# Casting v inside the load: GpSimd DMAs write bf16 into the block-diagonal operand of a windowed attention, ones on both sides of a row

## The chip, the cores and the metric

One core of one Trainium2 chip. The metric is the device time of one execution in microseconds, as the median of several runs. The profile is of one execution; its span runs from the first to the last instruction of the core.

## The reference

A causal sliding-window attention with a linear distance bias, followed by a spectral mixing over the sequence.

```python
# q, k, v: 8 batches, 8 heads, 576 tokens, 64 wide; fp32
scores = scale * q @ k.T                       # per batch and head
bias   = slopes[h] * -abs(i - j)               # slopes 2 ** (-(h + 1))
mask   = (i - j >= 0) & (i - j < 128)
attn   = softmax(where(mask, scores + bias, -1e9))
x      = (attn @ v) with heads side by side    # 8 x 576 x 512
X      = rfft(x, axis=1)[:, :64]               # 64 modes
Y      = X[:, m] @ (w_r[m] + 1j * w_i[m])      # a 512 x 512 pair for each mode
u      = x + irfft(Y, n=576)
out    = u + relu(u @ w_ch)                    # fp32
```

The 128 weight matrices w_r, w_i are 1 MB each in fp32, 134 MB together; q, k and v are 9.4 MB each, and so is the output.

## The kernel before

**Units and stages.** Attention works on 16 units, each one batch and four heads. The order on every engine is written out by hand: `STAGE` lists the steps of one stage with a lag in units, and the loop over stages runs through it, so that several units are in work at once. In one stage the casts of k run two units ahead, those of q three ahead, and the value matmuls and the norm one behind.

**Steps of a unit.** `load` issues DMAs from SP into fp32 buffers, two for each of q, k and v. `cast` turns them into bf16 on VectorE and issues the load of the unit two further on. q and k are transposed on PE (L250) and copied out by ScalarE (L256). `score` multiplies them (L284), `exp` runs on ScalarE (L294), `mask` multiplies two of the four tiles on VectorE (L305). `value` (L331) multiplies the exponentials with v; `norm` (L346, L347) takes the reciprocal of the row sums and scales the result into x. The accumulator `av` of the value matmuls has one buffer. `spectrum` and `channels` transform x into the modes, XC.

**The value operand.** Keys are taken in pairs of 128-key blocks, two keys to a partition (j = 0, 1). For a pair of blocks the operand vb has 2 x W columns with W = D + 2 = 66: partitions 0 to 63 hold v in the first W columns and zeros in the second, partitions 64 to 127 the other way round. Behind the 64 columns of v stand two columns of ones, so that the row sum comes out of the same matmul. The last 64 keys have an operand of their own, vt. `fixtures` writes the zeros and ones once, on GpSimd; the casts of v (L233 for both halves, L235 for the tail) write only the v columns. There are two vb and two vt.

**Loads of v.** Five DMAs a unit from SP: four with one head each (L208, 128 partitions, 2 runs of 512 bytes) and one for the tail (L212). They stand in SP's queue between the loads of q and k.

**Weights during attention.** `load_w` with bf16 issues a GpSimd DMA that reads fp32 and writes bf16. One such weight goes out per stage into the pool `early` (`AHEAD`, `EARLY` = 14 buffers); ahead of it GpSimd copies one element of x into `gate` (L533), which makes it wait for the norm of the stage. At the end of attention seven more weights go into the freed fp32 buffers of q, k and v (`spare`, `LATER`).

**The weight stream.** After attention the other weights come as fp32 from SP (L465) into `NWA` = 6 buffers and later `NWB` = 2 more; PE takes the upper halves of the fp32 words as bf16 (L838). Eight of the early buffers are loaded a second time by GpSimd (`AGAIN`). The inverse transform, the projection with w_ch and the outputs run beside it and at its end.

Of the kernel before, what the change touches and what calls it, by code (L numbers as in the profile page):

```python
# [10 lines left out]
FP32 = mybir.dt.float32  # L11
BF16 = mybir.dt.bfloat16
# [23 lines left out]


STAGE = (
    ("exp", 1, 0), ("score", 0, 0), ("exp", 0, 0), ("value", 0, 1), ("spectrum", None, 2),
    ("cast", "v", 0), ("score", 2, 0), ("channels", None, 2), ("transpose", "k", -1),  # L40
# [66 lines left out]
class _Attention:  # L107


    def __init__(self, tc, ctx, q, k, v, consts, x, XC, raw):  # L110
        self.tc, self.nc = tc, tc.nc
        self.q, self.k, self.v = q, k, v
        self.ident, self.F, self.FT = consts
        self.x, self.XC = x, XC
        B, H, S, _ = q.shape
        self.S, self.NG = S, H // 4
        self.units = [(b, g) for b in range(B) for g in range(self.NG)]
        self.raw = raw
        self.mid = ctx.enter_context(tc.tile_pool(name="amid", bufs=2))
        self.ps = ctx.enter_context(tc.tile_pool(name="aps", bufs=1, space=PSUM))  # L120
        fix = ctx.enter_context(tc.tile_pool(name="afix", bufs=1))
        self.table = fix.tile([P, H, 2, 2 * P], BF16, name="mask")
        self.bias = fix.tile([P, H, 2, 2 * P], BF16, name="bias")
        self.vb = [fix.tile([P, 2, 4, 2, 2 * W], BF16, name=f"vb{i}") for i in range(2)]
        self.vt = [fix.tile([P, 4, 2, W], BF16, name=f"vt{i}") for i in range(2)]
        self.qkT = [fix.tile([P, 2, 2, (FULL + 1) * P], BF16, name=f"qkT{i}") for i in range(2)]
        self.att = [fix.tile([P, FULL * 8 * P + 64], BF16, name=f"att{i}") for i in range(2)]
        self.loaded, self.casted, self.open = {}, {}, {}

    def fixtures(self, i):  # L130
        nc = self.nc
        for t, tail in ((self.vb[i], self.vt[i]),):
            for half in range(2):
                row = slice(64 * half, 64 * half + 64)
                c0 = W * half
                nc.gpsimd.memset(t[row, :, :, :, W - c0 : 2 * W - c0], 0.0)
                nc.gpsimd.memset(t[row, :, :, :, c0 + D : c0 + W], 1.0)
            nc.gpsimd.memset(tail, 0.0)
            nc.gpsimd.memset(tail[64:96, :, :, D:], 1.0)
        nc.gpsimd.memset(self.att[i][:, FULL * 8 * P :], 1.0)  # L140
# [57 lines left out]
    def load(self, w, u):  # L198
        nc = self.nc
        if u >= len(self.units):  # L200
            return
        b, g = self.units[u]
        hs = slice(4 * g, 4 * g + 4)
        if w == "v":
            t = self.raw[w][:, u % 2]
            sv = self.v[b, hs]
            for h in range(4):
                nc.sync.dma_start(  # L208
                    out=t[:, :2, h],
                    in_=sv[h, : FULL * P].rearrange("(r p j) d -> p r (j d)", r=2, j=2),  # L210
                )
            nc.sync.dma_start(  # L212
                out=t[64:96, 2],
                in_=sv[:, FULL * P :].rearrange("h (p j) d -> p h (j d)", j=2),
            )
        else:
            t = self.raw[w][:, u % 2]
            src = (self.q, self.k)["qk".index(w)][b, hs]
            nc.sync.dma_start(
                out=t.rearrange("p e j d -> p e (j d)"),  # L220
                in_=src.rearrange("(e h) (p j) d -> (h p) e (j d)", h=2, j=TPP),
            )
        self.loaded[w, u] = t

    def cast(self, u, w):

        nc = self.nc
        src = self.loaded.pop((w, u))
        if w == "v":
            src = src.rearrange("p s h (j d) -> p s h j d", j=2)  # L230
            for half in range(2):
                row = slice(64 * half, 64 * half + 64)
                nc.vector.tensor_copy(  # L233
                    self.vb[u % 2][row, :, :, :, W * half : W * half + D], src[row, :2])
            nc.vector.tensor_copy(self.vt[u % 2][64:96, :, :, :D], src[64:96, 2])  # L235
        else:
            dst = self.mid.tile([P, TPP, 2, D], BF16, tag=w, name=w)
            nc.vector.tensor_copy(dst.rearrange("p j e d -> p e j d"), src)
            self.casted[u, w] = dst
        self.load(w, u + 2)  # L240
# [66 lines left out]
    def value(self, u, e):  # L307
# [5 lines left out]
        att, vb, vt = self.att[u % 2], self.vb[u % 2], self.vt[u % 2]  # L313
        last = u == len(self.units) - 1 and e == 1
        av = self.ps.tile([P, 2, 512], FP32, tag="sc" if last else "av", bufs=2 if last else 1)
        for h in range(2):
            bank = av[:, h, : (FULL + 1) * W]
            todo = []
            for pair in range(2):
                rhs = [vb[:, pair, 2 * e + h, j] for j in range(2)]  # L320
                todo.append((pair, 0, 2 * pair, rhs))
                if pair == 1 and odd:
                    todo.append((pair, P, 3, [r[:, :W] for r in rhs]))
                    todo.append((pair, P - 64, 4, [r[:, W:] for r in rhs]))
                else:
                    todo.append((pair, P, 2 * pair + 1, rhs))
            todo.append((1, 192 - 64 * odd, 4, [vt[:, 2 * e + h, j] for j in range(2)]))
            for n, (pair, c0, qt, rhs) in enumerate(todo):
                for j in range(2):
                    o = (((2 * pair + h) * 2 + e) * 2 + j) * 256 + c0  # L330
                    nc.tensor.matmul(  # L331
                        bank[:, qt * W : qt * W + rhs[j].shape[1]],
                        lhsT=att[:, o : o + P], rhs=rhs[j],
                        start=(n == 0 and j == 0), stop=(n == len(todo) - 1 and j == 1),
                        skip_group_check=True,
                    )
        self.open["av", e, u] = av

    def norm(self, u, e):
# [6 lines left out]
        nc.vector.reciprocal(rec, tiles[:, :, :, D])  # L346
        nc.vector.tensor_tensor(  # L347
            out=self.x[:, b, :, cs].rearrange("p t (h d) -> p h t d", h=2),
            in0=tiles[:, :, :, :D],
# [50 lines left out]
def kernel(  # L400
# [14 lines left out]
    AHEAD = {stage: 1 for stage in range(1, 14)}  # L415
    LATER = {13: 2, 14: 2, 15: 3}
    EARLY, NWA, NWB, AGAIN = 14, 6, 2, 8
# [17 lines left out]
    raw["v"] = rawpool.tile([P, 2, 3, 4, 2 * D], FP32, name="vr")  # L435
    spare = [raw[w][:, i].rearrange("p e j d -> p (e j d)") for w in "qk" for i in range(2)]
    vflat = raw["v"].rearrange("p u s h d -> p (u s h d)")
    spare += [vflat[:, 2 * DM * i :] for i in range(3)]
    spare = [t[:, : 2 * DM].bitcast(BF16).rearrange("p (a e) -> p a e", a=4) for t in spare]
# [28 lines left out]
    with ExitStack() as actx:  # L468
        at = _Attention(tc, actx, q, k, v, (ident, F, FT), x, XC, raw)
        n = len(at.units)  # L470
        for w, u in (("q", 0), ("k", 0), ("q", 1), ("k", 1), ("v", 0), ("v", 1)):
            at.load(w, u)
# [19 lines left out]
        at.fixtures(0)  # L492
        load_w(1, early, True)
        next(table, None)
        at.fixtures(1)
        nc.gpsimd.memset(XC[:, 4 * NC * NM :], 0.0)
# [20 lines left out]
        run("cast", "v", 0)  # L517
# [461 lines left out]
```

## Time and profile before

| what | value |
|---|---|
| time of three runs | 444.14, 444.54 and 446.43 us, median 444.54 |
| span of the profiled execution | 441.7 us; its own time outside the span is not recorded, the median lies 2.8 us above it |
| PE busy | 332.8 us, 75% |
| DVE busy | 184.5 us, 42% |
| ACT busy | 162.1 us, 37% |
| POOL busy | 50.2 us, 11% |
| HBM read, written | 162.53 MB, 9.44 MB |
| attention | first q load at 0.74 us, last value matmul at 134 us |
| weight stream, first fp32 weight issued | 129.3 us |
| loads of v, median from issue to landing | 7.6 us |
| casted weights, median from issue to landing | 8.3 to 8.8 us |

Busy times are of each engine over the whole span; most of VectorE's and ScalarE's lies in the first third. A DMA that casts is counted by the bytes that it writes. "Landing" is the time at which the completion of a DMA is seen.

### The profile page before, as it was taken

Reading aid. Unit: us, or ns where it says so; the run is one execution under the profiler, and the core shown is the slowest. Engines: PE = TensorE matmul, PEld = TensorE weight load, DVE = VectorE, ACT = ScalarE, POOL = GpSimd, SP = SyncE. Lnnn points to the kernel's source line nnn. Section 1 sums busy time; section 2 is a strip of 40 time slices with the busy share of each in tenths; the row PEclk is TensorE's granted clock in tenths of the full one; section 3 lists DMA queues with packets and bytes.
Section 4 is the critical chain, followed back from the end, with each engine's and each line's share of the span. In section 5 each row is a group of like instructions: output and inputs, shape, how many; then the busy total and the mean of one; then the engine's idle time right before and its main releaser. Section 6 shows DMA issues by size and latency. Waiting matters only on the chain. (4 is left out here: it accounts for less than half of the span.)

```text
span 441.7 us, 8410 instructions
## 1 busy us (share of the span) xinstructions
PE 332.8 (75%) x3509; PEld 179.9 (41%) x3509; DVE 184.5 (42%) x332; ACT 162.1 (37%) x211; POOL 50.2 (11%) x107
## 2 busy tenths in 40 slices
PE   5589899879886454454545597999979999879982
PEld 4367677667664221121112133444434444333440
DVE  7789899887863200010000021332222223122694
ACT  6849899978960000000000011232222322101781
POOL 8711010101302200110000000000000000002500
PEclk9969999999998855555555569999999999999998
DMA  8999999999999999999999999999999999997498
GB/s 282 321 325 280 299 322 298 317 294 301 225 214 315 319 316 316 331 383 426 419 422 421 422 422 418 420 421 418 421 419 421 421 418 419 421 422 313 170 376 322
DMA packets 53209, 156.92 MB, mean 355 GB/s; under 512 B 4772, under 2 KB 23860, under 8 KB 40756
## 3 DMA queue, kind: packets, MB, share of 16 engines
q1 hardware_dynamic: 47860, 140.56, 82.2%
q0 software_dynamic: 5312, 15.84, 18.1%
q8 instruction: 27, 0.44, 0.4%
q14 instruction: 10, 0.08, 0.0%
HBM read 162.53 MB, written 9.44 MB: 389 GB/s over the span
## 5 line engine op out<-in xcount | busy, mean ns | idle before, releaser
L838 PE MATMUL acc<-w,XC 128*32 128x512 bf16 x456 | 93.1, 498 | 62.3 <-DMA w<-in_moe_w_r_dram 34.0
L838 PEld LDWEIGHTS <-XC 128*32 128x32 bf16 x508 | 39.4, 149 | 114.5 <-issue 100.1
L294 ACT ACTIVATE att<-sc 128x1024 bf16<-128x1024 f32 x64 | 64.1, 1032 | 10.7 <-PE sc L284 10.6
L604 ACT CAST ZW<-zw 128x512 bf16<-128x512 f32 x8 | 4.7, 585 | 147.6 <-PE zw L602 147.6
L331 PE MATMUL av<-vb,att 128*128 128x132 bf16 (+1 forms) x576 | 38.6, 218 | 10.9 <-DVE x L347 5.9
L331 PEld LDWEIGHTS <-att 128*128 128x128 bf16 x704 | 36.7, 99 | 16.3 <-DVE x L347 10.2
L576 DVE TENSOR_SCALAR yq<-acc 128x512 bf16<-128x512 f32 x14 | 9.6, 686 | 79.6 <-PE acc L838 79.6
L670 PE MATMUL my<-wch,xT 128*64 128x512 bf16 x288 | 34.5, 381 | 5.8 <-ACT x L701 4.3
L679 ACT CAST XW<-my 128x512 bf16<-128x512 f32 x36 | 19.3, 589 | 51.0 <-PE my L627 51.0
L651 DVE COPY xT<-tr 128x1024 bf16<-128x1024 bf16 x18 | 12.4, 691 | 55.0 <-PE tr L649 55.0
L256 ACT COPY qkT<-tp 128x1152 bf16<-128x1152 bf16 x30 | 33.5, 1116 | 2.8 <-PE tp L250 2.1
L616 POOL DMA_DIRECT2D Z<-yq x11 | 5.5, 511 | 217.4 <-issue 216.2
L347 DVE TENSOR_TENSOR x<-av,rec 128x640 bf16<-128x640 f32 x32 | 26.4, 824 | 1.1
L284 PE MATMUL sc<-qkT 64*64 64x256 bf16 (+2 forms) x640 | 25.1, 263 | 2.1 <-ACT qkT L256 1.2
L670 PEld LDWEIGHTS <-xT 128*64 128x64 bf16 x288 | 17.2, 109 | 21.7 <-issue 9.3
L794 DVE TENSOR_TENSOR o<-yy,r 128x1024 f32<-128x1024 f32 (+1 forms) x22 | 21.5, 1024 | 4.3 <-ACT r L770 3.2
L233 DVE CAST vb<-vr 64x1024 bf16<-64x1024 f32 x32 | 22.6, 708 | 0.2
L701 ACT CAST x<-my 128x512 bf16<-128x512 f32 x18 | 10.5, 585 | 33.0 <-PE my L627 33.0
L284 PEld LDWEIGHTS <-qkT 64*64 64x64 bf16 x640 | 14.5, 109 | 19.4 <-issue 16.3
L702 DVE CAST x<-my 128x512 bf16<-128x512 f32 x18 | 12.4, 691 | 23.4 <-PE my L627 23.4
L271 PE MATMUL sc<-bias,ident 128*128 128x512 bf16 x64 | 20.8, 409 | 1.3 <-ACT att L294 1.3
L305 DVE TENSOR_TENSOR att<-att,mask 128x1024 bf16<-128x1024 bf16 x32 | 20.6, 683 | 0.0
(130 smaller groups left out, 396.6 us busy)
## 6 DMA issues: line engine op xcount, KB each, us to landing
w<-in_moe_w_i_dram SPq DMA_DIRECT2D x49, 1024.0 KB, 17.9
w<-in_moe_w_r_dram SPq DMA_DIRECT2D x48, 1024.0 KB, 16.0
qr<-in_q_dram SPq DMA_DIRECT2D x16, 576.0 KB, 10.3
kr<-in_k_dram SPq DMA_DIRECT2D x16, 576.0 KB, 8.6
vr<-in_v_dram SPq DMA_DIRECT2D x64, 128.0 KB, 7.6
out_dram<-o SPq DMA_DIRECT2D x13, 512.0 KB, 4.5
w<-in_moe_w_r_dram POOLq DMA_DIRECT2D x12, 512.0 KB, 8.8
w<-in_moe_w_i_dram POOLq DMA_DIRECT2D x10, 512.0 KB, 8.3
```

The lines of the kernel that those rows point to most:

```text
L233: nc.vector.tensor_copy(self.vb[u % 2][row, :, :, :, W * half : W * half + D], src[row, :2])
L256: (self.nc.vector.tensor_copy if u < 2 and w == "q" else self.nc.scalar.copy)(dst.rearrange("q h (p j) -> q h p j", j=TPP), tp.rearrange(" ...
L271: nc.tensor.matmul(sc[:, e], lhsT=self.ident, rhs=self.bias[:, hv].rearrange("p j n -> p (j n)"), start=True, stop=False, skip_group_check ...
L284: nc.tensor.matmul(sc[64 * half : 64 * half + 64, e, j * 256 + c0 : j * 256 + c0 + n], lhsT=qkT[row, 1, h, k0 + j : k0 + P : 2], rhs=qkT[r ...
L294: self.nc.scalar.activation(self.att[u % 2][:, kt * 8 * P : (kt + 1) * 8 * P], sc.rearrange("p e n -> p (e n)"), AF.Exp, scale=1.0 / math. ...
L305: nc.vector.tensor_tensor(out=rows, in0=rows, in1=self.table[:, heads], op=ALU.mult)
L331: nc.tensor.matmul(bank[:, qt * W : qt * W + rhs[j].shape[1]], lhsT=att[:, o : o + P], rhs=rhs[j], start=(n == 0 and j == 0), stop=(n == l ...
L347: nc.vector.tensor_tensor(out=self.x[:, b, :, cs].rearrange("p t (h d) -> p h t d", h=2), in0=tiles[:, :, :, :D], in1=rec.unsqueeze(-1).br ...
L670: nc.tensor.matmul(mm[ROWS[half]], lhsT=lhsT, rhs=wch[:, dt], start=(dt == 0), stop=False, skip_group_check=True,)
L679: nc.scalar.copy(XW[:, j, n], mms[n])
L794: nc.vector.tensor_tensor(out=o[:, c], in0=yy[:, c], in1=r[:, c], op=ALU.add)
L838: nc.tensor.matmul(into[32 * (m % 4) : 32 * (m % 4) + 32], lhsT=XC[:, c0 : c0 + 31 * NM + 1 : NM], rhs=wq[t][a], start=(ri == 0 and a == 0 ...
```

## The change

v is no longer loaded as fp32 and cast on VectorE. GpSimd DMAs read fp32 from HBM and write bf16 straight into vb and vt, five a unit as before: one for each pair of blocks and half (64 partitions, four heads, 128 elements each) and one for the tail. So that a run of 128 elements (two keys) can stand in one piece, a row is now [1, v of key 0, v of key 1, 1], WV = 130 columns: the matmul of key 0 takes the first 65, that of key 1 the last 65, shifted by one column in the accumulator. The sums of the two keys then lie in columns 0 and 65 of W = 66, and `norm` adds them with a tensor_reduce before the reciprocal. vb has three buffers (NV) instead of two, held where the fp32 buffers of v were, and vt three. The load of unit u + 3 is issued behind the second half of the value matmuls of unit u. The fixtures of the three buffers are written ahead of their first loads. One weight more is loaded early (15 instead of 14, two in stage 7), the spare buffers are filled in other stages, and the fp32 buffers are split 5 and 3 instead of 6 and 2.

```diff
+NV = 3
+WV = 2 * D + 2
 STAGE = (
-    ("cast", "v", 0), ("score", 2, 0), ("channels", None, 2), ("transpose", "k", -1),
+    ("score", 2, 0), ("channels", None, 2), ("transpose", "k", -1),
...
-        self.vb = [fix.tile([P, 2, 4, 2, 2 * W], BF16, name=f"vb{i}") for i in range(2)]
-        self.vt = [fix.tile([P, 4, 2, W], BF16, name=f"vt{i}") for i in range(2)]
+        self.vb = raw["v"]
+        self.vt = [fix.tile([P, 4, WV], BF16, name=f"vt{i}") for i in range(NV)]
...
     def load(self, w, u):
...
         if w == "v":
-            t = self.raw[w][:, u % 2]
+            t = self.vb[:, u % NV]
             sv = self.v[b, hs]
-            for h in range(4):
-                nc.sync.dma_start(
-                    out=t[:, :2, h],
-                    in_=sv[h, : FULL * P].rearrange("(r p j) d -> p r (j d)", r=2, j=2),
-                )
-            nc.sync.dma_start(
-                out=t[64:96, 2],
+            for half in range(2):
+                row = slice(64 * half, 64 * half + 64)
+                for r in range(2):
+                    k0 = (2 * r + half) * P
+                    nc.gpsimd.dma_start(
+                        out=t[row, r, :, half, 1 : WV - 1],
+                        in_=sv[:, k0 : k0 + P].rearrange("h (p j) d -> p h (j d)", j=2),
+                    )
+            nc.gpsimd.dma_start(
+                out=self.vt[u % NV][64:96, :, 1 : WV - 1],
                 in_=sv[:, FULL * P :].rearrange("h (p j) d -> p h (j d)", j=2),
             )
+            return
...
     def cast(self, u, w):
-        if w == "v":
-            ...
-                nc.vector.tensor_copy(
-                    self.vb[u % 2][row, :, :, :, W * half : W * half + D], src[row, :2])
-            nc.vector.tensor_copy(self.vt[u % 2][64:96, :, :, :D], src[64:96, 2])
...
     def value(self, u, e):
...
+                m = rhs.shape[1]
+                dst = bank[:, qt * W : (qt + m) * W].rearrange("p (m w) -> p m w", w=W)
                 for j in range(2):
                     nc.tensor.matmul(
-                        bank[:, qt * W : qt * W + rhs[j].shape[1]],
-                        lhsT=att[:, o : o + P], rhs=rhs[j],
+                        dst[:, :, j : j + D + 1],
+                        lhsT=att[:, o : o + P], rhs=rhs[:, :, j * (D + 1) : (j + 1) * (D + 1)],
...
+        if e == 1:
+            self.load("v", u + NV)
     def norm(self, u, e):
-        nc.vector.reciprocal(rec, tiles[:, :, :, D])
+        nc.vector.tensor_reduce(out=rec, in_=tiles[:, :, :, 0 : D + 2 : D + 1],
+                                axis=mybir.AxisListType.X, op=ALU.add)
+        nc.vector.reciprocal(rec, rec)
...
-    AHEAD = {stage: 1 for stage in range(1, 14)}
-    LATER = {13: 2, 14: 2, 15: 3}
-    EARLY, NWA, NWB, AGAIN = 14, 6, 2, 8
+    AHEAD = {stage: 1 + (stage == 7) for stage in range(1, 14)}
+    LATER = {13: 2, 14: 3, 15: 1, 16: 1}
+    EARLY, NWA, NWB, AGAIN = 15, 5, 3, 8
...
-    raw["v"] = rawpool.tile([P, 2, 3, 4, 2 * D], FP32, name="vr")
+    raw["v"] = rawpool.tile([P, NV, 2, 4, 2, WV], BF16, name="vb")
...
-        for w, u in (("q", 0), ("k", 0), ("q", 1), ("k", 1), ("v", 0), ("v", 1)):
+        for w, u in (("q", 0), ("k", 0), ("q", 1), ("k", 1)):
...
         at.fixtures(0)
+        at.load("v", 0)
         load_w(1, early, True)
         next(table, None)
         at.fixtures(1)
+        at.load("v", 1)
+        at.fixtures(2)
+        at.load("v", 2)
```

## The prediction

> **What bounds the kernel now.** I read the page's slices first, to see which resource is full where, then its queues, then the stage windows, and last who waits for whom.
>
> ```profile
> DVE  7789899887863200010000021332222223122694
> ACT  6849899978960000000000011232222322101781
> DMA  8999999999999999999999999999999999997498
> GB/s 282 321 325 280 299 322 298 317 294 301 225 214 315 319 316 316 331 383 426 419 422 421 422 422 418 420 421 418 421 419 421 421 418 419 421 422 313 170 376 322
> ```
>
> A slice is 11 us. The DMA row is 9 or more from the second slice to the 36th, through attention (slices 1 to 12) as through the weight stream behind it. So two things must be told apart in attention, where VectorE and ScalarE are at 7 to 9 tenths too: does the arithmetic set the pace, or the transfers? The GB/s row seems to speak for arithmetic (300 against 420), but it counts what is written, and a GpSimd DMA that casts writes half of what it reads.
>
> ```profile
> q1 hardware_dynamic: 47860, 140.56, 82.2%
> q0 software_dynamic: 5312, 15.84, 18.1%
> ```
>
> The casting queue took 18.1% of the engines' time for 15.84 MB, 198 GB/s written, which is 396 read. So I go by time per packet, from the trace's packet records (set to the span's start). A 512-byte packet of v takes 27 ns (median; mean 30.4), a 2304-byte packet of q or k 95 (103), an 8192-byte fp32 weight packet 313, a casting packet 8192 to 4096 bytes 322. Successive packets overlap by a few ns, so the engine's own price comes from stretches with one kind alone: 637 packets of v in 10.0:11.0 is 16/0.637 = 25 ns, 92 of q and k in 21.5:22.0 is 87 ns, and weights alone, cast or not, run at 424 GB/s, 309 ns per 8192 bytes.
>
> One unit of attention moves 512 packets of q and k, 1152 of v and 128 of one casted weight: (512x87 + 1152x25 + 128x309)/16 = 2.78 + 1.80 + 2.47 = 7.05 us. The gate copies on GpSimd, one per stage, are 7.37 us apart (27.38 to 115.80 in 12 stages). Transfers fill 96% of a stage. From 125 us on the same prices fill all of it.
>
> ```profile
> 27.40:40.00 12.60, 12.02 (x206) 9.23 (x206) 10.73 (x20) 11.54 (x12) 2.16 (x4) 0.92 1.05 277
> 40.00:115.80 75.80, 67.56 (x1238) 52.24 (x1236) 65.08 (x117) 66.61 (x76) 8.93 (x20) 0.98 1.08 302
> 115.80:125.00 9.20, 8.33 (x149) 6.09 (x147) 6.72 (x13) 8.42 (x10) 3.63 (x7) 1.00 1.01 205
> 190.00:400.00 210.00, 161.66 (x1094) 68.66 (x1093) 42.24 (x84) 33.37 (x60) 0.00 (x0) 0.83 1.01 419
> ```
>
> Columns: window, its length, busy PE, PEld, DVE, ACT, GpSimd, clock, DMA share, GB/s. Priced by packet, the 36.9 us of 3.1:40 hold 33.3 us of transfer, the 75.8 us of 40:115.8 hold 73.1, the 9.2 us of 115.8:125 hold 7.8. The losses are 3.6 + 2.7 + 1.4 = 7.7 us, and after 125 nothing is lost until the last weight at 405. The bytes do not change. So the change can win at most these 7.7 us plus what v's packets get cheaper; what VectorE saves is worth nothing by itself.
>
> **The change part by part.**
>
> *VectorE.* The rows of the casts and of the division:
>
> ```profile
> L233 DVE CAST vb<-vr 64x1024 bf16<-64x1024 f32 x32 | 22.6, 708 | 0.2
> L347 DVE TENSOR_TENSOR x<-av,rec 128x640 bf16<-128x640 f32 x32 | 26.4, 824 | 1.1
> ```
>
> 32 x 0.708 = 22.6 us and the tails' 16 x 0.412 = 6.6 go. 32 tensor_reduce of 128x20 from PSUM come, which the trace does not have: above the reciprocal of 128x10 (0.216), below L347 (0.824); by the reciprocal, near in size, 0.23, so 7.4 us. The reciprocal then reads SBUF: 0.216 kept. Net -21.8 us, 1.36 us a unit. The reduce lengthens the chain from the value matmuls to the release of their one accumulator, for which PE now waits 16 us in all, by 0.23 us; but the cast of v (1.8 us) that stood ahead of the first norm of each stage is gone. Nothing lost on this chain.
>
> *SP.* 80 issues go. They stand between the loads of q and k, and SP waits there:
>
> ```profile
> SPq L208 <- DMA qr<-in_q_dram: 17.1, 11, 2.5
> SPq L208 <- DVE vt L235: 11.8, 7, 3.5
> ```
>
> q and k are then issued as soon as a cast frees their buffer. Off the path, but it keeps the engines fed.
>
> *GpSimd.* 80 issues come, five a unit: four of 256 runs, one of 128. A weight of 128 runs takes 0.55 us to issue, the 512 runs of wch 0.76; I take 0.60 and 0.55, 2.95 us a unit. Behind them stand the gate copy and the weight's issue of the same stage. The cover is the 83.8 us that GpSimd waits at the gate, 5 to 8 us a stage; without it the 2.95 us would delay each weight. A new wait is each v load's wait for the value matmuls three units earlier; what stands behind it, one weight, is prefetch. A further one is the semaphore of the eighth issue before, 1.3 stages earlier, with landings of 8 us: no stall, or a short one.
>
> No issue of a DMA in the trace falls beside a cast on VectorE, but the second set of fixtures does: its memsets take 1.43 and 0.73 us beside the casts of v from 13.7 to 16.6, against 0.97 and 0.27 alone, 0.46 more each. If all five issues of a unit met a cast, they would take 5.3 us; with gate and weight (1.1) that is 6.4 of the 7.37, still hidden.
>
> [...]
>
> *Start.* The first v leaves SP at 2.77 now; after, it waits for the fixtures on GpSimd (to 11.36) and then 3 to 5 us for its first packet (the first weight: issued 11.36, first packet 16.87). The third set of fixtures costs 5.3 us (12.98 to 18.28) before the third v. Against this q and k of the third and fourth units go out some 5 us earlier. By 40 us I count the same transfers done as now, 33 us' worth: zero, with -2 to +4 as bounds.
>
> *v's packets*, the term that decides: 18,432 of 512 bytes now, the same 18,432 runs read after, but cast to 256 bytes written. The trace has no such packet. Lower end: at the weights' rate of 26.5 bytes a ns, 512 bytes read are 19.3 ns, 5.7 less than 25: -6.6 us. Upper end: casting packets take 322 ns for 4096 bytes written and 96 for 1024 (wch), a line of 20.6 ns + 0.0736 per byte, 39.5 ns for 256; 12.5 more than 27, +14.4 us if nothing of it overlaps. I take 0: casting weights alone reach the same 424 GB/s as plain ones though their packets last 9 ns longer, so the cast is latency and not occupancy, and v reads as much as before.
>
> [...]
>
> *End of attention.* Now the last casted weights wait for v's casts (GpSimd 7.5 us at L459) in the stretch that loses 1.4 us. After, four weights are issued at once behind the last gate, 12 us of transfers with the gate's own, and only the last three wait for value matmuls. I take back 1.2 us.
>
> *Steady stages.* The 2.7 us of 40:115.8 come from engines short of work or packets hindering each other; with q and k no longer behind v I take half, 1.3 us.
>
> *One answer.* Two columns fewer in 448 matmuls of 225 ns: 1.5 us off PE, beside transfers. One casted weight more and a 5+3 instead of 6+2 split of fp32 buffers: same bytes and same count of eight, in a stretch that is full.
>
> Sum: 0 (v) + 0 (start) - 1.2 - 1.3 = -2.5 us on the profiled span of 441.7, to 439.2. The runs' median of 444.54 has 2.8 us around that span, which stay: 442.0 us. Own range 438.5 to 443.5. A difference under 0.5%, 2.2 us, can't be told from none on this kernel.
>
> **The rivals.**
>
> *Casting small packets occupy the engine longer* (slower). Place: v's 1152 packets in each of 16 units; price up to 12.5 ns each, 0.9 us a unit, 14.4 in all. It decides once a third of it shows ((2.5+2.2)/14.4). For it: both casting rows are longer than plain ones. Against: the 424 GB/s. Most likely near two thirds, 442.0 + 9.6 = 451.6; all of it 456.4.
>
> *v comes late* (slower or same). v of the third unit is issued about 29 to 32 and lands at 36 or 37, while its matmuls start at 35.7 now; if GpSimd stays behind, transfers thin out at the start by up to 4 us: 446.
>
> *Nothing is won back.* The 4% lost in a stage are packets hindering each other whatever the queue: 444.5.
>
> *Runs of v go through several to a packet*, at the weights' rate: -6.6 more, 435.4.
>
> **How the numbers follow.** Forecast 0.46, of it 0.33 below 442.3 and 0.13 above. Slow casting packets 0.24 (0.22 slower, 0.02 same). v late 0.10 (0.07 slower, 0.03 same). Nothing won 0.12 (0.10 same, 0.02 slower). Cheaper packets 0.08, faster. So faster 0.41, same 0.28, slower 0.31. The range reaches from most of the cheap case, 436, to most of the dear one, 455.
>
> **What would show it.** Right: 18,432 packets on the software queue at about 27 to 39 ns with gates still 7.1 to 7.3 us apart; DMA at 9 in every slice to the 36th; VectorE at 6 to 7 tenths in attention; SP's waits at L208 gone. Wrong: gates 8 us apart with a full DMA row (packets dearer); DMA below 9 in slices 2 to 4 with PE waiting for v (v late); GpSimd busy all through a stage (issue dearer than 0.6 us). A sum that holds in attention with a longer end would put the fault in the 5+3 buffers.

## The result and the profile after

| | before | after |
|---|---|---|
| median time, us | 444.73 (444.14 to 446.43, 4 runs) | 463.37 (460.94 to 466.12, 4 runs) |
| ratio, 95% interval | 1 | 1.0408 (1.0377 to 1.0438) |
| profiled span, us | 441.7 | 461.7 |
| VectorE busy, us | 184.5 | 163.8 |
| GpSimd busy, us | 50.2 | 102.6 |
| last value matmul starts, us | 134.0 | 151.7 |
| from there to the end of the span, us | 307.7 | 310.0 |

The change is 4.1% slower: 18.6 us by the medians, 20.0 us by the two spans. Attention takes nearly all of it. The slices of the page after, in the same four rows as before:

```profile
DVE  7646566652655221100000011322223222212594
ACT  6846796974796000000000002222212222201681
DMA  8999999999999999999999999999999999998498
GB/s 305 223 271 166 236 233 247 221 249 250 150 141 188 313 316 281 318 322 372 425 419 422 422 420 421 421 419 419 422 419 420 420 420 417 420 422 357 147 364 322
```

The DMA row is as full as before (9 from the second slice on), but VectorE and ScalarE have fallen to 5 to 7 tenths: the DMA engines set the pace and get less done. The queues show where the work went:

```profile
q1 hardware_dynamic: 28004, 130.07, 72.8%
q0 software_dynamic: 25168, 21.09, 31.2%
```

v's 18,432 packets are now on the casting queue. The windows of attention, then one of the weight stream (window, length, busy PE, PEld, DVE, ACT, GpSimd, clock, DMA share, GB/s):

```profile
27.40:40.00 12.60, 6.73 (x84) 4.94 (x83) 4.86 (x10) 4.49 (x5) 7.39 (x13) 0.68 1.32 191
40.00:115.80 75.80, 57.65 (x1024) 45.60 (x1031) 42.42 (x87) 56.55 (x63) 32.64 (x60) 0.92 1.19 235
115.80:125.00 9.20, 8.36 (x143) 6.76 (x147) 5.53 (x13) 6.53 (x8) 6.77 (x11) 0.91 1.18 150
190.00:400.00 210.00, 154.85 (x1055) 64.92 (x1056) 39.44 (x81) 31.67 (x58) 2.80 (x8) 0.78 1.02 409
```

From 40 to 115.8 us PE does 1024 matmuls instead of 1238. A DMA share above 1 counts packets that are in flight together; it was 1.08 and is 1.19. The weight stream reaches the same rate as before (slices of 417 to 425 GB/s); the 409 of the window, against 419, is its slower beginning, which now falls inside. The gate copies, from the view of their line:

```profile
L543 POOL COPY gate<-x x13: 176/178/795, 40.2 to 138.2; 1x1 bf16<-1x1 bf16 x13
```

The first stands at 40.2 instead of 27.4, and they are (138.2 - 40.2)/12 = 8.17 us apart instead of 7.37. The waits:

```profile
DVE rec L350 <- PE av L333: 53.1, 30, 9.3
POOL vb L214 <- DMA vb<-in_v_dram: 21.2, 15, 2.3
PE av L333 <- DMA vb<-in_v_dram: 16.2, 8, 7.5
POOL vb L214 <- PE av L333: 12.8, 8, 3.1
```

```profile
SPq L226 <- DVE k L237: 43.0, 13, 5.4
SPq L226 <- DVE q L237: 40.0, 13, 9.0
```

PE waits 16.2 us for v, VectorE 53.1 us for PE, and SP, with v off its queue, for the casts that free the buffers of q and k. GpSimd waits 21.2 us at the issue of a v load for the landing of one issued earlier (the one issued at 73.74 us stood until the eighth issue before it had landed, at 73.46); in the trace before GpSimd stands so once, for 4.5 us ahead of wch. The groups of the new division and of v's loads:

```profile
L350 DVE TENSOR_REDUCE rec<-av 128x10 f32<-128x20 f32 x32 | 5.7, 178 | 53.1 <-PE av L333 53.1
L353 DVE TENSOR_TENSOR x<-av,rec 128x640 bf16<-128x640 f32 x32 | 26.4, 824 | 1.1
L214 POOL DMA_DIRECT2D vb<-in_v_dram x64 | 41.9, 660 | 50.3 <-DMA vb<-in_v_dram 21.2
```

The casts of v are gone, the reduce takes 178 ns, and an issue of 256 runs 660 ns on the mean. From issue to landing a v load takes 9.9 us (7.6 before), a casted weight 12.7 to 13.3 (8.3 to 8.8).

**A ledger of bytes.** Between 200 and 400 us the kernel before lands weights at a steady 0.42 MB a us (from 46.7 to 130.6 MB). What is not moved by the end of attention is paid for there, at that rate. So each run below is read by the megabytes of q, k, v and weights (counted as read from HBM) that its packet records show as landed: by 40 us, in the steady stretch 40 to 120, and in the end of attention, 120 to 160. Times of packets are on the trace's own clock, on which the last packet ends 1.3 us before the span does; the packet times of the prediction, and the 55.9 and 57.0 MB in the expectation of `aligned_turns`, stand 1.3 us too late, as if it ended with the span.

| run | ratio to before | by 40 | 40 to 120 | 120 to 160 | by 160 | short by, us | span longer by, us | v packet mean, ns |
|---|---|---|---|---|---|---|---|---|
| before | 1 | 13.2 | 29.3 | 16.8 | 59.3 | 0 | 0 | 30.4 |
| after | 1.0408 | 11.5 | 26.1 | 13.5 | 51.1 | 19.6 | 20.0 | 49.0 |
| before_halves | 1.0536 | 11.8 | 23.5 | 13.8 | 49.1 | 24.3 | 25.5 | 46.5 |
| after_turns | 1.0323 | 11.4 | 26.4 | 14.5 | 52.3 | 16.6 | 18.9 | 43.7 |
| after_start | 1.0404 | 11.6 | 25.5 | 13.2 | 50.2 | 21.6 | 21.3 | 51.0 |
| after_inner | 1.0158 | 11.2 | 28.9 | 15.0 | 55.1 | 10.0 | 11.1 | 41.6 |
| aligned | 1.0119 | 12.1 | 29.2 | 15.2 | 56.5 | 6.7 | 7.8 | 41.7 |
| aligned_start | 1.0157 | 12.1 | 28.7 | 14.9 | 55.7 | 8.6 | 9.0 | 41.4 |
| aligned_turns | 1.0113 | 12.1 | 28.8 | 14.8 | 55.7 | 8.6 | 9.0 | 41.8 |
| whole | 1.0068 | 12.0 | 29.4 | 16.2 | 57.5 | 4.2 | 5.5 | 41.5 |
| staged | 1.0064 | 12.4 | 29.2 | 16.8 | 58.4 | 2.2 | 3.0 | 41.0 |
| staged3 | 0.9909 | 13.1 | 30.4 | 16.8 | 60.4 | -2.5 | -1.9 | 40.9 |

"Short by" is the missing megabytes over 0.42 MB a us. It foretells every span within 2.3 us: the ledger is a good account of where the time goes, and the question is what makes less move.

### The profile page after: what moved, and what is told of

Same layout as the page of the kernel before. It is cut to its first block, busy times and chain, and to the rows that moved or that the text cites. A ratio compares the mean times of both kernels' runs of the same rounds, so it can differ in the third digit from the quotient of the medians.

```text
span 461.7 us, 8376 instructions
## 1 busy us (share of the span) xinstructions
PE 333.4 (72%) x3488; PEld 182.3 (39%) x3509; DVE 163.8 (35%) x316; ACT 161.9 (35%) x211; POOL 102.6 (22%) x194
## 5 line engine op out<-in xcount | busy, mean ns | idle before, releaser
L848 PE MATMUL acc<-w,XC 128*32 128x512 bf16 x456 | 91.3, 509 | 58.1 <-DMA w<-in_moe_w_i_dram 28.7
L848 PEld LDWEIGHTS <-XC 128*32 128x32 bf16 x508 | 39.1, 148 | 115.1 <-issue 94.0
L293 ACT ACTIVATE att<-sc 128x1024 bf16<-128x1024 f32 x64 | 64.1, 1032 | 13.8 <-PE sc L283 13.6
L333 PE MATMUL av<-vb,att 128*128 128x130 bf16 (+1 forms) x576 | 42.2, 225 | 24.0 <-DMA vb<-in_v_dram 16.2
L214 POOL DMA_DIRECT2D vb<-in_v_dram x64 | 41.9, 660 | 50.3 <-DMA vb<-in_v_dram 21.2
L333 PEld LDWEIGHTS <-att 128*128 128x128 bf16 x704 | 39.4, 102 | 31.1 <-issue 14.9
L661 DVE COPY xT<-tr 128x1024 bf16<-128x1024 bf16 x18 | 12.4, 692 | 56.9 <-PE tr L659 56.9
L283 PE MATMUL sc<-qkT 64*64 64x256 bf16 (+2 forms) x640 | 25.5, 266 | 5.6 <-ACT qkT L255 1.6
L353 DVE TENSOR_TENSOR x<-av,rec 128x640 bf16<-128x640 f32 x32 | 26.4, 824 | 1.1
L680 PEld LDWEIGHTS <-xT 128*64 128x64 bf16 x288 | 17.1, 109 | 21.8 <-issue 9.3
L350 DVE TENSOR_REDUCE rec<-av 128x10 f32<-128x20 f32 x32 | 5.7, 178 | 53.1 <-PE av L333 53.1
L804 DVE TENSOR_TENSOR o<-yy,r 128x1024 f32<-128x1024 f32 (+1 forms) x22 | 21.6, 1025 | 4.5 <-ACT r L780 3.1
L712 DVE CAST x<-my 128x512 bf16<-128x512 f32 x18 | 12.4, 691 | 21.8 <-PE my L637 21.8
## 6 DMA issues: line engine op xcount, KB each, us to landing
w<-in_moe_w_r_dram SPq DMA_DIRECT2D x48, 1024.0 KB, 16.2
w<-in_moe_w_r_dram POOLq DMA_DIRECT2D x12, 512.0 KB, 12.7
w<-in_moe_w_i_dram POOLq DMA_DIRECT2D x11, 512.0 KB, 13.3
```

Of the source, the lines that this page charges most:

```text
L214: nc.gpsimd.dma_start(out=t[row, r, :, half, 1 : WV - 1], in_=sv[:, k0 : k0 + P].rearrange("h (p j) d -> p h (j d)", j=2),)
L283: nc.tensor.matmul(sc[64 * half : 64 * half + 64, e, j * 256 + c0 : j * 256 + c0 + n], lhsT=qkT[row, 1, h, k0 + j : k0 + P : 2], rhs=qkT[r ...
L293: self.nc.scalar.activation(self.att[u % 2][:, kt * 8 * P : (kt + 1) * 8 * P], sc.rearrange("p e n -> p (e n)"), AF.Exp, scale=1.0 / math. ...
L333: nc.tensor.matmul(dst[:, :, j : j + D + 1], lhsT=att[:, o : o + P], rhs=rhs[:, :, j * (D + 1) : (j + 1) * (D + 1)], start=(n == 0 and j = ...
L353: nc.vector.tensor_tensor(out=self.x[:, b, :, cs].rearrange("p t (h d) -> p h t d", h=2), in0=tiles[:, :, :, 1 : D + 1], in1=rec.unsqueeze ...
L661: nc.vector.tensor_copy(xTs[j], tr)
```

## The experiments

### Bursts: what does one packet of v cost?

```diff
+# one of the forms; loops over batches, halves and r left out
+# 4096 runs of two keys of v, in one form after another, nothing else running
+queue.dma_start(out=t[row, i, r, :, hf, 1:129], in_=s[:, k0 : k0 + P].rearrange("h (p j) d -> p h (j d)", j=2))
```

> This kernel computes nothing of the reference: it loads v in ten bursts of 4096 runs of two keys each, one form after the other, each waiting for the one before, and writes zeros. Theory 1 (dear packets): a packet that reads 512 bytes and writes 256 by a cast holds its DMA engine for 40 ns or more once the burst lasts, so its burst takes 10 us or more where the plain 512-byte form takes 6.4 to 8 (25 to 31 ns); the forms between (cast or plain, 64 or 128 partitions, write at a multiple of 32 bytes or shifted by 2 bytes, 256 or 512 bytes written) say which property does it. Theory 2 (late queue): all bursts of 512-byte reads sustain 25 to 31 ns, whatever is written, and the loss lies in the order and the semaphores of GpSimd's queue.

In this first set a burst could overlap the next; in the second each was ended by a pass of VectorE over its tile.

> Bursts of 4096 runs of v again (two keys each), each burst now ended by a VectorE pass over its whole tile, in nine forms: whole 128 partitions and 64-partition halves in fp32 by SP; the change's casting DMAs (64-partition halves, 2 bytes off, rows of 130); the same on rows of 144 with the run at element 16; the change's form with every DMA on partitions 32 to 95; the change's form with the two halves alternating; both keys of a pair of rows as one run of 1024 bytes cast; plain 256-byte runs by SP on halves, aligned and 2 bytes off. Compute left out, output zeros. [...] Rival 'the rows of 130 or the bank, not the partitions': partitions 32 to 95 stay at 40 or more. Rival 'the first burst's price was only its overlap with the next': the change's form falls to 28 to 30.

Time of a burst x 16 engines / 4096 runs:

| form (read to written bytes) | set | ns a run | GB/s written |
|---|---|---|---|
| SP, 512 to 512, 128 partitions | 2 | 30.4 | 270 |
| SP, 512 to 512, 64-partition halves | 2 | 40.3 | 203 |
| cast 512 to 256, 128 partitions, aligned | 1 | 27.1 | 151 |
| cast, 128 partitions, 2 bytes off | 1 | 27.5 | 149 |
| cast, halves, aligned rows of 144 | 2 | 32.3 | 127 |
| cast, halves, 2 bytes off, rows of 130 (the change) | 2 | 47.8 | 86 |
| the same, every DMA on partitions 32 to 95 | 2 | 30.9 | 133 |
| the same, lower and upper halves in turn | 2 | 39.1 | 105 |
| SP, 256 to 256, 128 partitions, aligned / 2 bytes off | 1 | 18.5 / 25.4 | 221 / 161 |
| SP, 256 to 256, halves, aligned / 2 bytes off | 2 | 23.3 / 43.5 | 176 / 94 |

Each row is one burst of one execution. The first set also has the change's form, at 45.1, and plain fp32 runs from GpSimd: 31.0 on whole partitions, 40.7 on halves, as from SP.

The cast costs nothing (27.1 against 30.4), nor does the shift of a casted run on whole partitions (27.5); a plain 256-byte run pays 6.9 ns for it. Halves and shift together cost 17 ns more than the load before. That it is not the number of partitions, nor the rows of 130, shows in the row of 32 to 95: 64 partitions, shifted, in rows of 130, and 30.9 ns. Halves in turn came to 39.1. And it is not the casting queue: plain fp32 halves from SP are dearer by 9.9 ns, plain shifted halves by 25.

Where the 64 partitions lie matters: halves of 0 to 63 and 64 to 127 bring plain runs from 270 to 203 GB/s, and the change's form falls from 47.8 to 30.9 ns when only the place of its partitions changes. But the change's form writes 86 GB/s, far under 203, so no single rate for halves gives its price. The runs show what the shift costs (18.5 to 25.4 ns, on halves 23.3 to 43.5), not why. A plain 256-byte run on whole partitions takes 18.5 ns against 30.4 for one of 512, 221 GB/s written against 270.

### aligned, before_pool, no_v: three ways to take one part away

`aligned` keeps all of the change but starts v's run at a multiple of 32 bytes:

```diff
+PV, OV = 144, 15   # row pitch, first element: v then starts at element 16
...
-    raw["v"] = rawpool.tile([P, NV, 2, 4, 2, WV], BF16, name="vb")
+    raw["v"] = rawpool.tile([P, NV, 16 * PV + 16], BF16, name="vb")
```

> The changed kernel with rows of 144 elements and v at element 16, so that every run of v is written to a multiple of 32 bytes instead of 2 bytes beside one. If the shift by 2 bytes is what makes v's packets dear: 444 to 450 us. If it is the cast, the 256 bytes, the half partitions or the queue: 461 to 465, as the change.

1.0119 (1.0081 to 1.0156), 450.12 us. Without the shift 13 of the 18.6 us are gone and the steady stretch moves 29.2 MB. Aligned halves write 127 GB/s in the bursts (32.3 ns a run), well under the 203 that halves reached with fp32 (40.3 ns).

`before_pool` is the kernel before with its fp32 loads of v issued by GpSimd:

```diff
-                nc.sync.dma_start(
+                nc.gpsimd.dma_start(
```

> The kernel before with nothing changed but the queue of v: the same five loads a unit, fp32 to fp32, issued by GpSimd ahead of its weight instead of by SP; the casts stay on VectorE. Theory 2 (late queue: eight semaphores for six issues a stage, GpSimd waiting in order): v is late as in the change, 455 to 465 us. Theory 1 (dear packets): 512-byte writes as before, 443 to 448 us.

1.0211 (1.0180 to 1.0241), 453.91 us, but this does not price the queue alone: the loads, issued first on GpSimd, put off the identity and the tables (first value matmul 30.8 instead of 23.8 us), and SP's 512-byte runs become 4096-byte packets on GpSimd's queue, as in the first bursts (1024 packets for 8192 runs). In the bursts such packets sustain 31.0 ns a run, no dearer than from SP. `staged` below keeps the tables early and tests queue and cast together.

`no_v` issues no load of v after unit 2:

```diff
-        if e == 1:
-            self.load("v", u + NV)
```

> The changed kernel without the loads of v behind the third unit; the value matmuls of later units use the v that is there. If all of the loss lies in the loads of v, 13/16 of it goes (15 us), and 13 units of plain v at 1.80 us each on top (23 us): 425 us. If the loss lies in the other edits (5 and 3 fp32 buffers, the order of the last casted weights), only the 23 us go: 440 us.

0.9946 (0.9908 to 0.9985), 443.34 us: nearer to the 440 that was expected if the loss lay in other edits than to 425. It does not decide this, since with 7.7 MB less to move attention gains little over the kernel before: its gates come 7.06 us apart. The weights moved by 160 us are the same 31.0 MB as before, because one weight is let go per stage. Its steady window:

```profile
40.00:115.80 75.80, 68.18 (x1274) 53.96 (x1282) 53.77 (x110) 68.97 (x77) 12.13 (x23) 0.98 0.87 223
```

DMA engines have room (0.87), ScalarE and PE are busy for 91% and 90%: it looks as if a stage had a second limit, 4% under the first, though no run speeds up those engines to show it. A transfer that gets cheaper could then gain little here, while a dearer one sets the pace.

### after_start, aligned_start: is it the late start of v?

The first gate comes 12.8 us later after the change, so I tried to take the start away: zeros of buffers 1 and 2 by VectorE, and the loads of units 0 to 2 back to back, ahead of the first weight and the table steps.

```diff
+        for i in (1, 2):
+            at.zeros(i, nc.vector)
...
-        at.fixtures(0)
+        at.zeros(0, nc.gpsimd)
+        at.ones(0)
         at.load("v", 0)
-        load_w(1, early, True)
-        next(table, None)
-        at.fixtures(1)
+        at.ones(1)
         at.load("v", 1)
-        at.fixtures(2)
+        at.ones(2)
         at.load("v", 2)
+        load_w(1, early, True)
+        next(table, None)
```

> The change, with the zeros of its second and third buffer written by VectorE before the tables, the ones of all three buffers and the DMAs of units 0, 1 and 2 issued back to back on GpSimd, and the first weight load and the table steps behind them. Theory 'v's late arrival at the start is worth some 8 us of the 18.6': the first stage weight is cast at 30 to 32 us instead of 40, stages stay 8.0 to 8.2 apart, the run takes 453 to 456. Rival 'the start is caught up later by weights that would have been early, so it costs 3 us or less': 459 to 463 whatever the first gate does.

> Both: rows of 144 with v at element 16, and v's DMAs early as in the run before. If the two terms are separate and add up (6 to 8 us of start, 13 of alignment), 441 to 444, at or just under the kernel before; stages 7.2 to 7.4 apart, the first at 30 to 32. If the start's cost was only a consequence of slow packets, 448 to 450 as with aligned rows alone.

1.0404 (1.0323 to 1.0485), 463.08 us, and 1.0157 (1.0098 to 1.0216), 452.22 us: nothing gained. My theory of 8 us of start fell. The second unit's last value matmul starts at 38.3 us instead of 42.9, as before the change (38.6), but that of the tenth at 112.4 against 115.0 and the last of all at 152.3 against 151.7. The early units only waited later: from 40 to 120 us `after_start` moves 25.5 MB, the change 26.1.

### whole, after_inner: the same DMAs on other partitions

`whole` sends the same 18,432 casted, shifted runs in four DMAs by head, each on all 128 partitions (the zeros and ones are placed to match; partitions 64 to 127 then hold the wrong keys, the value matmuls take 219 ns in the median, as with the change):

```diff
-            for half in range(2):
-                row = slice(64 * half, 64 * half + 64)
-                for r in range(2):
-                    nc.gpsimd.dma_start(out=t[row, r, :, half, 1 : WV - 1], ...)
+            for h in range(4):
+                nc.gpsimd.dma_start(
+                    out=t[:, :, h, 0, 1 : WV - 1],
+                    in_=sv[h, : FULL * P].rearrange("(r p j) d -> p r (j d)", r=2, j=2))
```

> The change with its four half-partition DMAs of 256 runs replaced by four DMAs by head of 256 runs on all 128 partitions (all into block 0, still 2 bytes off, rows of 130), so that bytes, runs, packets and issues are the same; the block-diagonal operand then holds the wrong keys (the output is not the reference's), the matmuls are unchanged. Theory 'half the partitions times an off-by-two write': packets fall from 49 to about 40 ns on average, stages 7.2 to 7.5 apart instead of 8.17, run 449 to 453. Rival 'off-by-two alone, or the casting queue itself': stages stay 8.0 to 8.2, run 460 to 464.

1.0068 (1.0023 to 1.0114), 449.25 us. From 40 to 120 us it moves 29.4 MB, before 29.3. The steady window, to be held against the second line of the windows after:

```profile
40.00:115.80 75.80, 66.10 (x1257) 52.48 (x1262) 54.19 (x109) 67.96 (x77) 43.56 (x71) 1.00 1.20 255
```

1257 matmuls instead of 1024. The DMA share is 1.20, as with the change (1.19): the share does not tell slow packets from packets in flight, the work done does.

By taking one head per DMA `whole` also reads v in another order. `after_inner` does not: it leaves the DMAs as they are, 64 partitions each, and moves them to 32 to 95 (the other partitions hold constants):

```diff
-                row = slice(64 * half, 64 * half + 64)
+                row = slice(32, 96)
```

> The change with one thing moved: all four of its half DMAs write partitions 32 to 95 (four different blocks of the operand) instead of 0 to 63 and 64 to 127. Same shape, bytes, 2-byte shift, rows, queue and order; the other partitions hold constants, so the output is not the reference's, and the matmuls are the same. The fixtures take some 1.5 us longer. Theory 'which partitions a DMA writes sets the price' (30.9 against 47.8 ns in the bursts): like whole partitions, 448 to 451, stages 7.1 to 7.3 apart, packets 41 to 42 ns on the mean. Rival 'a DMA on 64 partitions is dear wherever they lie' (fewer partitions, more runs on each): 460 to 465, packets near 49 ns.

1.0158 (1.0117 to 1.0198), 454.00 us: 9 us better than the change by the medians, 11 by the ratios, and 3 above what I expected. v's packets take 41.6 ns on the mean instead of 49.0, as with whole partitions, and the steady stretch moves 28.9 MB. The rest lies mostly at start and end: 11.2 MB by 40 us, the least of all (six of its memsets write 64x1040 in place of 64x16; in the trace after these sizes take 1.00 and 0.18 us), and 15.0 from 120 on.

```profile
40.00:115.80 75.80, 63.90 (x1153) 49.22 (x1142) 47.77 (x97) 61.64 (x70) 40.65 (x74) 0.95 1.20 256
```

### before_halves, after_turns, aligned_turns: halves without a cast, halves in turn

`before_halves` puts the half-partition form into the kernel before, fp32, aligned, from SP:

```diff
-            for h in range(4):
-                nc.sync.dma_start(
-                    out=t[:, :2, h],
-                    in_=sv[h, : FULL * P].rearrange("(r p j) d -> p r (j d)", r=2, j=2))
+            for half in range(2):
+                row = slice(64 * half, 64 * half + 64)
+                for r in range(2):
+                    k0 = (2 * r + half) * P
+                    nc.sync.dma_start(
+                        out=t[row, r],
+                        in_=sv[:, k0 : k0 + P].rearrange("h (p j) d -> p h (j d)", j=2))
```

> The kernel before, still fp32 from SP and cast on VectorE, but v's four DMAs of 256 runs each write 64 partitions (as in the change) instead of 128. No cast in the DMA, no 2-byte shift, no GpSimd. Theory 'writing half the partitions is dear by itself' (40.3 ns a packet against 30.4 in the bursts, 9.9 ns x 18,432 / 16 = 11.4 us, of which two thirds showed for the change's packets): 451 to 456, v's packets near 40 ns. Rival 'only casting or shifted writes suffer, or only GpSimd's queue': 443 to 446.

1.0536 (1.0479 to 1.0592), 469.0 us: slower than the change itself, with no cast, no shift and no GpSimd. The direction is settled; the size is more than twice the 6 to 11 us that I expected. v's packets take 46.5 ns on the mean against 30.4 (16.1 x 18,432 / 16 = 18.5 us), and q's and k's, untouched, 122.6 against 103.0 (19.6 x 8192 / 16 = 10.0 us): other packets, here on the same queue, are slowed too. Why 46.5 here and 40.3 in a burst is open.

```profile
40.00:115.80 75.80, 55.96 (x999) 43.45 (x996) 50.28 (x90) 54.27 (x61) 5.64 (x16) 0.95 1.09 237
```

`after_turns` swaps two loops of the change, so that neighbouring DMAs go to different halves; `aligned_turns` does the same on aligned rows.

```diff
-            for half in range(2):
-                row = slice(64 * half, 64 * half + 64)
-                for r in range(2):
+            for r in range(2):
+                for half in range(2):
+                    row = slice(64 * half, 64 * half + 64)
```

> The change with two loops of its load swapped: lower and upper half of a pair of blocks are issued in turn instead of both lower halves first. The same four DMAs, the same bytes, partitions and addresses, another order. [...] Rival 'the price hangs on the packet alone (cast, shift), not on what is written beside it': 461 to 464.

> Aligned rows (pitch 144, v at element 16) and the halves in turn. If what is left of aligned rows over whole partitions (450.1 against 449.3 us, 55.9 against 57.0 MB by 160 us) is the halves, 448 to 450; if it is start and end of attention alone, 450 as with aligned rows.

1.0323 (1.0254 to 1.0393), 461.24 us: v's packets fall to 43.7 ns and the steady stretch moves 26.4 MB instead of 26.1, but the interval overlaps that of the change, and the gain is 2 us by the medians and 4 by the ratios, where the bursts (39.1 against 47.8 ns, 8.7 x 18,432 / 16) promised 10. Unclear. 1.0113 (1.0069 to 1.0158), 451.16 us: as aligned rows. Since turns hardly helped the shifted rows in this kernel, this does not tell whether the halves are part of what is left there.

### staged, staged3: the cast in the DMA without the halves

The kernel before, with GpSimd DMAs that cast v into dense bf16 buffers on 128 partitions, and VectorE copying bf16 where it cast:

```diff
-    raw["v"] = rawpool.tile([P, 2, 3, 4, 2 * D], FP32, name="vr")
+    raw["v"] = rawpool.tile([P, 4, 3, 4, 2 * D], BF16, name="vr")
...
-                nc.sync.dma_start(
+                nc.gpsimd.dma_start(     # u % 4, loaded three units ahead
```

> The kernel before with only its loads of v changed: GpSimd casts them into dense bf16 buffers on all 128 partitions (four buffers, loaded three units ahead), and VectorE copies bf16 to bf16 into the block-diagonal operand where it cast fp32 before. Value matmuls, norm, fixtures, weights' buffers and stages as before. From the bursts a casted run on whole partitions takes 27.1 ns against 30.9 for a plain one, 3.8 x 18,432 / 16 = 4.4 us less at most, two thirds of it 2.9; the start, where the change and its variants had moved 1 MB less by 40 us, may cost up to 2.4. Theory 'the packets were the whole damage, and the cast in the DMA is free': 440 to 445, stages 7.1 to 7.3 apart. Rival 'loads of v on GpSimd cost by themselves' (issues, semaphores, the queue): 448 to 452.

1.0064 (1.0042 to 1.0086), 447.38 us. All 18,432 runs are casted in the DMA and the steady stretch moves 29.2 MB: the cast is not what costs. The 0.9 MB that it is short by 160 us are nearly all missing by 40 us (12.4 against 13.2). GpSimd, which no longer has time to spare at the gate, waits:

```profile
POOL vr L208 <- DMA vr<-in_v_dram: 12.1, 14, 1.3
POOL vr L208 <- DMA w<-in_moe_w_r_dram: 6.4, 4, 2.0
POOL vr L208 <- DMA w<-in_moe_w_i_dram: 6.2, 4, 2.3
```

Five loads and a weight a unit, and each issue waits for the landing of one issued earlier, the weight in front of the next load included: 24.7 us. `staged3` merges the four loads by head into two by r, of 512 runs each:

```diff
-            for h in range(4):
+            for r in range(2):
                 nc.gpsimd.dma_start(
-                    out=t[:, :2, h],
-                    in_=sv[h, : FULL * P].rearrange("(r p j) d -> p r (j d)", r=2, j=2),
+                    out=t[:, r],
+                    in_=sv[:, 2 * r * P : 2 * (r + 1) * P].rearrange("h (p j) d -> p h (j d)", j=2),
```

> The run with dense bf16 staging and VectorE copies, its four DMAs of 256 runs a unit merged into two of 512 (three issues a unit with the tail, instead of five). Theory 'its remaining 2.7 us are GpSimd waiting, at the semaphore of the eighth DMA before, for landings': with three issues and a weight a unit the eighth lies two units back, those waits (vr waiting for w and vr, 24.7 us) all but go, and the run takes 442 to 445, at best 0.5% under the kernel before. Rival 'what is left is the start, where v comes later than from SP, or the end of attention': 446 to 448, waits gone and time the same.

0.9909 (0.9882 to 0.9937), 441.9 us against 446.01 beside it: 0.9% faster than the kernel before, more than the 0.5% expected at best, and the only complete version that beats it. Its waits:

```profile
POOL gate L537 <- DVE x L347: 33.3, 11, 6.2
POOL vr L208 <- DMA vr<-in_v_dram: 10.7, 8, 2.4
```

The waits of v's loads for weights are gone, 10.7 of the 24.7 us stay, GpSimd has time to spare at the gate again (33.3 us), and all three columns of the ledger are at or above those of before but for 0.1 MB by 40 us. The merging does two things at once: it takes away waits, and it shortens the issues at the start, so that the first gate stands at 30.5 us instead of 35.9. Of the 2.0 MB over `staged` by 160 us, 0.7 are there by 40 us and 1.2 come in the steady stretch; which of the two does how much was not tried apart.

## Why the prediction was wrong, point by point

442.0 us was predicted, with 455 as the top of the range; 463.4 came.

**Right: the frame.** Transfers bound the kernel, and VectorE's time is worth nothing by itself: VectorE was rid of 20.7 us of work (predicted 21.8; the tensor_reduce takes 178 ns, not 230) while the time rose. SP's waits went as said: its loads of q and k now wait for VectorE's casts (43.0 and 40.0 us). The first line of "what would show it wrong" is what happened: gates 8 us apart with a full DMA row.

**The step that failed: v's packets, taken at 0.** I priced a packet by the bytes that it reads and by its cast, and never looked at where it writes. The argument about the cast was right: the line through the casting packets gave 39.5 ns, the packets take 41, and `staged3`, with the same packets and faster than before, shows that this is latency and costs no time. But the change also went from 128 partitions to halves and from aligned to shifted runs, which the diff shows plainly. Between `whole` and the change only the four DMAs differ, in the partitions that they write and in the order in which they read v: 1.0408 - 1.0068 = 0.034, 15 us. `after_inner`, where only the partitions differ, wins 11 us back, and `aligned`, where only the shift goes, 13: for casted runs it takes both to lose the time. Why the two together cost so much stays open. That the 15 us are close to the upper bound of 14.4 is chance; the bound was worked out from casting, and for the same reason the rival with the dear packets had the right size of price and the wrong mechanism.

**Start, taken at 0** (bounds -2 to +4): by 40 us 1.7 MB less is moved, 4.1 us; with cheap packets (`whole`) 1.2 MB, 3.0 us. That is at the upper bound, on the side of the rival "v comes late". Its sign, PE waiting for v, showed (16.2 us), but `after_start`, with v early and the time the same, shows that the late start is not where the time is lost.

**End of attention, taken at -1.2:** wrong sign. `whole` moves 0.6 MB less than before from 120 to 160 us, 1.5 us lost. The last weights wait there for value matmuls to free v's buffers (7.8 us); that this is the cause was not tried alone.

**Steady stages, taken at -1.3:** `whole` gives 0 within 0.3 us. Only `staged3` moves more than before (30.4 against 29.3 MB, 2.6 us).

**GpSimd.** The issue was priced at 0.60 us and takes 0.66, no matter. The wait for the eighth issue before was called "no stall, or a short one": it is 21.2 us for v's landings alone. Landings became slower (a weight's 12.7 to 13.3 us, before 8.3 to 8.8) just as issues became more. From `staged` to `staged3` 5 us are won by the spans and 7 by the ratios (1.0064 against 0.9909); the waits are worth that at most, since the start gained too.

With the ledger of `whole`, packets 15.1, start 3.0 and end 1.5 make 19.6 us, against 18.6 measured. `whole` keeps all other edits, the 5 and 3 buffers among them, so together these cost no more than its own 0.7%. The range ended at 455 because it took the dearest packet with everything else at its best.

**Two readings that were off.** The prediction's packet times are 1.3 us late (the first weight's first packet comes at 15.61 us, not 16.87, 4.2 us after its issue); prices per packet do not depend on it. And it read that no issue of a DMA falls beside a cast: one does, at 109.20 us, beside a cast of q, and takes 0.66 us where most take 0.53.

**Issues beside casts.** After the change an issue and a cast of k stand side by side like this:

```profile
84.17 0.95 POOL L214 DMA_DIRECT2D vb<-in_v_dram  x1 [1.82 <-DMA vb<-in_v_dram]
84.22 0.75 DVE L237 CAST k<-kr 128x1152 bf16<-128x1152 f32 x1
```

Of the 64 issues of 256 runs seven lie beside a cast for 0.66 us or more. Each of them ends 144 to 148 ns after the cast does and takes 0.81 to 1.26 us, where the median of all is 0.62; eight that a cast touches for less than 0.4 us take 0.61 to 0.65. That is 2.5 us more in the whole of attention; all five issues of a unit beside a cast, at the prediction's 0.46 us more each, would be 2.3 us a unit, but most issues meet no cast.

## What to carry to other kernels

Price a DMA by what it writes as well as by what it reads: which partitions, and on which byte a run starts; for casted runs two costs that are small alone (27.5 and 32.3 ns) made 47.8 together, and for fp32 runs halves alone cost 24 us (`before_halves`). Where the DMA engines are the bound, count megabytes moved by the end of the phase and read every variant against that, since waits and first arrivals shift without adding to the sum (`after_start`: 50.2 MB by 160 us, the change 51.1). If a layout needs halves, let the DMA write whole partitions densely and let an engine that has the time place the halves (`staged3`, 0.9909); use few and large DMAs where each issue waits for an older landing (24.7 us of such waits in `staged`, 10.7 in `staged3`).

## What the runs showed of the hardware that was not expected

- For casted runs 2 bytes off, DMAs on partitions 32 to 95 are nearly as fast as on 128 (30.9 against 27.5 ns a run), on 0 to 63 and 64 to 127 they are not (47.8).
- Where v's writes were slow, other packets were longer in flight too: those of q and k rose from 103.0 to 124.4 ns after the change, with v on another queue, and to 122.6 in `before_halves`, with v on theirs.
- GpSimd's queue merges plain 512-byte runs into 4096-byte packets (`before_pool`; in the first bursts 1024 of its 20,064 packets carry 8192 such runs), casting ones not (18,432 packets of 256 bytes written after the change).
- A casting packet of 512 to 256 bytes is in flight for 41 ns after the change, against 27 of a plain one before (medians), and 18,432 of them cost no time in `staged3`.
- An issue on GpSimd that lies beside most of a cast of q or k on VectorE ends some 145 ns after the cast: up to 1.26 us instead of 0.62.
